# Last group's value product of a SwiGLU block as seven block products, in a planned single-core kernel

## The chip, the cores and the metric

The kernel runs on one core of a Trainium2 chip. The metric is the device time of one execution in microseconds (us); the time of a kernel is the median of several such executions.

## What is computed

Attention with two kinds of heads, and behind it a SwiGLU block on its output. The reference, cut to what matters:

```python
batch, n_heads, seq, head_dim = (4, 8, 768, 64)
n_sink, window = (4, 64)                     # heads 0, 2 and 6: causal
keep = causal & (is_sink | in_win)           # the other five heads
a = softmax(where(mask, q @ k.T / 8, -1e9))
attn_out = a @ v
x = attn_out.transpose(0, 2, 1, 3).reshape(3072, 512)
g = x @ w_gate                               # 512 x 1536
silu = g * (1.0 / (1.0 + np.exp(-g)))
val = x @ w_val                              # 512 x 1536
out = (silu * val) @ w_out                   # 1536 x 512
```

All inputs and the output are float32.

## The kernel before

The 3072 tokens are 24 tiles of 128, and four tiles make a group of 512 tokens: six groups, g = 0 to 5. Attention works on pairs of tiles: q and k are cast to float16 (`copy`, lines 206 on ACT and 208 on DVE and POOL, `recast`, line 212) and transposed by TensorE (line 473); then scores (line 567), exponentials on ACT (line 579), masks (line 587, DVE or POOL), values (line 597), the division by the row sums (lines 604 and 605, DVE), and a DMA that transposes the result into `xt`, the layout that the SwiGLU block takes.

For each group there are twelve blocks j of 128 of the 1536 columns. `gate` (line 759) makes four 512-wide matmuls into a PSUM bank, once with `wg_sb` (the gate) and once with `wv_sb` (the value, called vals). ACT takes the tanh of half the gate (line 765), and DVE makes two passes: `stt1` (line 769), sil = (tanh + 1) * gate, and `stt2` (line 775), h = 0.5 * sil * value, which goes as float16 into `h_sb`. `stt1` reads `sig` from SBUF and the gate from PSUM; `stt2` reads `sil` from SBUF and the value from PSUM.

The out projection h @ w_out is already done in 2x2 blocks with seven block products in all six groups (`seventh`, line 860: twelve 256-wide matmuls for each product). With A the blocks of h (token halves by column halves) and W those of w_out, it needs four sums of blocks of h (`hsum`, line 831, each in two parts, on DVE or POOL; named hs4.1.0 for group 4, sum 1, part 0) and four of w_out, made once (`wsum`, line 412). The products p1 to p7 of a group come together again in `gathered` (a copy at line 890, sums with a cell of `out_sb` at line 898); stores follow at lines 908, 911 and 919. The last group ends with its products in the order p1, p7, p6, first half of p2, p5, p4, second half of p2, the two halves of p3.

Nothing is scheduled at run time. The kernel's text adds tasks with their dependencies, and three tables, made beforehand by a planner, say what happens: `ORDER` (two base-62 digits for each task, in the order in which the tasks are issued; numbers of 3700 and above are matmuls that fill), `WAYS` (which of a task's engines takes it) and `SLOTS` (which buffer of a ring or which PSUM bank it uses). Each engine works through its own instructions in that order, and semaphores hold it until what it needs is there. The rings have 11 buffers `raw` (128x1024 float32, the landing place of the loads), 3 `sil`, 2 `sig`, 2 `xt`, and 8 PSUM banks that gates, values and products share.

The places that the change and the prediction touch:

Of the kernel before, what the change touches and what calls it, by code (L numbers as in the profile page):

```python
# [16 lines left out]
    "06000307090A0401081U0D1V1cy11W1X0C1d1f1e0B2021021g280g1i2229231h2B2A1j0m1r2C0h1Y1p1s2D1a0F1Z2N1q"  # L17
    "2X1b1k2E0G2O1l2W1t1m2F1u2L1x1v1w2f2M1n2g2c1y1oxk2h0n27242d25262e2l2i2m2G1z0E0y2H2I2P0z2Q2j8e2R2t"
    "8o0k8f112o2x8p8g302p108q2U312J0i132V8h2K8r2y050H8t8s8y8i8u2k983C8w8v8m323D8j2n2z3I0q8k9D8x991493"
    "3J8l9A3L8z8n94380l91903K96950o2Z9E929B3M979G2Y9F0I3N9C3U339H1C3R3V2a2q2r0j342b9h2s3S162u3O3W9c9i"  # L20
    "0r3T3X9j359d363b9I3P0J3E372v9J3Q3f3i1D2w9N9e0K1F3A9O9f3B3g2S3H9k0p179P3G0v9m9g393F9l9Q9n3h0s3Y3j"
    "9K3Z0u199r3u3a3c3n9R0x3l9s401G3k3m0w9L3o0L3d9M9S3v419o9u2T9t0M9T3p429U433w3q9v441A9p3r450R4C493e"
    "1B469q4A9X4H3y3s4B9Y9a479Z9V3t4D9b3x4Q4N4K9W4OAu9z480O4LAQ9y1H18AnA00tB2Av124RAz1EAw0P4EB0A1BE4Z"
    "B1Ap4V4Y4gB34FBH4GBF0NAxAq1Q1K4hBGAV5CArAkAWBIB41IAl0QAX1J15AY4eAy1S4IB7AZAm0SALAR3z4JAoB51MAs4d"
    "AS9wAt4f1RAM5DANB91TB69x5KBCB8BA4b5fBBAa0WBD5I4o4i4l4P4pA2A45l4m1LA34M5FAT0U1N5E4S5L1PAUAf4jA5A8"
    "1OAg4v5JAbAh4a4k4TAcAE5g4UA95n4y514q4c4zAAA60V4r0a6KACAB5o5GA7AF4WAdAD524n4sAGAiAeAK540TAj505T55"
    "4t5mAO4u5U5MAP565W4x5753AHBM4wBLBJBN5NAI5c5VAJ58595XBO4XBR5A5H5O5BBK5v5p5sBP5wBX5q5Y0YBQ600Z5r5Z"
    "5t5a0XBV5b6I5u6366BWCb6E6HBS645iCe5h6N67BY5PBTCC6O5QBbCD5R7O5d6PCM6wCc6v5xCd0cBZ68CECN71BcCF6JBa"
    "5SCP65BdCf5yCH72COCGBsBUCI73CJ69Bv6A5z5j0fBt6R616U74BuBi6V6e7RC7Bw0bBj6W5kBkCW6zCQ706B6CCX7SBlC8"
    "6D6SCAC96GBmC2CY7P6QCKC3CB6LCZ6T6x5e6yC4BnCLBhBqBoCa82626FBxBpBr7U6X7F6ZBy7GC0Bz0eCiCR6aC10d6Y7C"  # L30
    "7W6nCS75BeCT767XC5Bf776b6cBg6oDj6d7QDm7DC685DtDk7ED5DuDlCUD86gCVDvDUCk7VDeDnDVD6Cj78DwD7ClDXDWDf"
    "Dx79DA7LDY7HDPDgD9CgDQ7A80DR7B7b6kCmDBDh6lDCDSDi7c6MCh7Y6h817Z6p7jDyDT877a7I7J6q6mDK8883DzDD7K6f"
    "DoE07NDLCoDMDp6iCn86DEE16j89CsE2Cp6rCt7m7e7n6sDqDF7M7f7oCuDGDNCv7dDH7gCw6tCqDO6u7s7pCx7t7h7xDZ7i"
    "7q7T8D8ADa8G7rCyDb8H7k8E8NDI84Cz8B8F7uD07v8Y8I7wDc8C8J8ZDJ8T8W7y8Q8XEzDdCr8K8L8UEX8MDr8OEw7lD1Ex"
    "8P8REyF9D2D4F0F6D38SF1F7DsEh8VF88aE58bE6FJFAFB8cE7FE8dFCEiErEj7zE3FDF2E8FFFGFLFHFIEkFKEYEcF3EaEA"
    "EdElF4EZEBEbE4EmE9EEG9EnF5EeFOEoFMEfEDEsEuEtGMEvEFFNEgEpEGGJEHGKGLESEqEIGEG4GFGGGHG5FPEJGIG6G7EC"
    "GTG8GCGUGAEOGBEKETEVEUGiEWGWGjGVELFuENFTGNFxFvGXERGlFSGkFpEMFwFVGYFqGDFQEPFrGOFyFsGPFRGQGREQFUGZ"
    "GdGmFWFYGaFXFzFtFbGSGbG0GeG1G2FaFiG3FZFcGfGpGcGgFdFeGrGhFlGqFfFjFgFmGsFnGnFhFkGzGoGtFoGuGvGxH7Gy"
    "H3GwH8H9H0H1H4HAH6H2HDHBH5HCHGHEHFHHHI"
)  # L40
WAYS = (
    "000000000000000000000000000000000000000000000000000000000000222212202202222022110100101101110001"
    "212100001000000000000000210012022201011011000000000000001100222212001010000000000001000000000000"
    "001200002201000000000001000000001000000010000000000220120000000000010000002000000000000020000220"
    "000000100100000000200010000000000020000000000000000000000000210002120000000000100000210001001000"
    "002202020020000001001000000002000000000000000021002000000000000000010001000202220000000001000000"
    "000010010000010002212100000010010000000100000000000000000000000000000000000000000000000000000000"
    "000000000000000000000000000000000000000000001100001100000000000000000000000000000000000000000000"
    "000000000000000000000000000000000000000110000000000000000000000000000000000000000000000000000000"
    "000000000000000000010001100011000000000001000000000000000000000000000000000000000000000000000000"  # L50
    "000000001000000000000000000000110000000000000000000000000000000000000000000000000000000000000011"
    "010000110000000000010000000000000000000000000000000000000000000000000000000000000000101000000000"
    "00011001011000000"
)
# [1073 lines left out]
```

## Time and profile before

| what | value |
|---|---|
| median of 3 executions | 239.04 us (238.83 to 239.19) |
| profiled execution | 239.03 us |
| span in its profile | 237.2 us |
| PE (TensorE matmuls) busy | 230.5 us, 97% |
| DVE (VectorE) busy | 194.5 us, 82% |
| ACT (ScalarE) busy | 141.2 us, 59% |
| POOL (GpSimd) busy | 110.6 us, 47% |
| moved by DMA | 40.73 MB |

The profile is one execution seen by the hardware profiler. Its times are in us. PE is the sequence of matmuls and PEld that of weight loads, which overlap them; SP issues most of the DMAs. A row of the timeline gives the start, the duration, the engine, the line of the kernel, the operation with its output and inputs, and in brackets how long the engine had waited and for what. A row of a group of instructions gives their busy time, the mean duration in ns, and the idle time before them with what ended it. A row of stretches gives the busy time of PE, PEld, DVE, ACT and POOL, each with its instructions, then the granted clock of TensorE (1.00 is full speed), the busy share of the DMA engines and GB/s.

### The profile page before, as it was taken

How to read it: one execution, taken by the hardware profiler on the slowest of the kernel's cores; microseconds unless marked ns; L12 is line 12 of the kernel's file. 1: busy time of each engine (PE TensorE's matmuls, PEld its weight loads, DVE VectorE, ACT ScalarE, POOL GpSimd, SP SyncE). 2: the span in 40 equal slices, each digit the busy share in tenths (PEclk: the TensorE clock that was granted, in tenths of full speed). 3: DMA queues.
4: the chain of work that ended last, by engine and by line, in shares of the span. 5: the costliest groups of instructions: out<-in, count | busy, mean ns of one | idle time of the engine just before them, and what ended most of it. 6: DMA issues, size and time to landing. Idle time of an engine off the chain costs nothing.

```text
span 237.2 us, 5639 instructions
## 1 busy us (share of the span) xinstructions
PE 230.5 (97%) x2211; PEld 146.0 (62%) x2211; DVE 194.5 (82%) x362; ACT 141.2 (59%) x217; POOL 110.6 (47%) x132
## 2 busy tenths in 40 slices
PE   7899999999999999999999999999999999999994
PEld 2577865655457778655464557766555565557883
DVE  2689999998999699698968989786969867788873
ACT  3699999889599879839575485384242232231010
POOL 7386577937484940998600550884000000525500
PEclk9999999999999999999999999999999999999999
DMA  6999999999999999999798124011620000220044
GB/s 173 351 343 366 326 346 356 358 350 296 271 238 165 236 291 182 289 164 188 196 171 207 34 48 87 4 22 20 203 44 0 3 0 0 87 92 1 20 183 155
DMA packets 67194, 40.73 MB, mean 172 GB/s; under 512 B 25184, under 2 KB 61024, under 8 KB 67168
## 3 DMA queue, kind: packets, MB, share of 16 engines
q1 hardware_dynamic: 65248, 37.50, 63.4%
q10 hardware_dynamic: 1920, 2.88, 3.3%
q8 instruction: 17, 0.28, 0.5%
q14 instruction: 9, 0.07, 0.1%
HBM read 28.31 MB, written 6.29 MB: 146 GB/s over the span
## 4 chain that ended last, share of the span: by engine, by line
PE 92%; DVE 3%; DMA 2%; ACT 1%; issue 0%; DVEq 0%
PE banks L759 51%; PE banks L860 23%; PE banks L567 8%; PE banks L597 6%; PE banks L473 2%; DMA raw<-in_q_dram 2%; PE banks L621 1%; DVE wt_sb L412 1%; DVE sil L769 1%; ACT hq L206 0%; PE banks L321 0%; DVE kT L208 0%; DVE hq L212 0%; DVE qT L208 0%; DVE xb L605 0%; DVE h_sb L775 0%
## 5 line engine op out<-in xcount | busy, mean ns | idle before, releaser
L765 ACT ACTIVATE sig<-banks 128x512 f32<-128x512 f32 (+1 forms) x76 | 42.7, 574 | 54.6 <-PE banks L759 47.5
L759 PE MATMUL banks<-xt,wg_sb 128*128 128x512 f16 (+1 forms) x304 | 71.4, 368 | 0.5 <-DVE sil L769 0.5
L759 PE MATMUL banks<-xt,wv_sb 128*128 128x512 f16 (+1 forms) x304 | 70.9, 368 | 0.0
L579 ACT ACTIVATE e<-banks 128x1024 f16<-128x1024 f32 (+2 forms) x68 | 59.5, 910 | 15.0 <-PE banks L567 6.3
L769 DVE SCALAR_TENSOR_TENSOR sil<-sig,banks 128x512 f32<-128x512 f32 (+1 forms) x76 | 48.8, 655 | 14.3 <-ACT sig L765 13.6
L775 DVE SCALAR_TENSOR_TENSOR h_sb<-sil,banks 128x512 f16<-128x512 f32 (+1 forms) x76 | 48.9, 655 | 2.8 <-PE banks L759 1.8
L860 PEld LDWEIGHTS <-h_sb 128*128 128x128 f16 x420 | 40.4, 98 | 8.5
L759 PEld LDWEIGHTS <-wv_sb 128*128 128x128 f16 x304 | 28.6, 98 | 26.9
L759 PEld LDWEIGHTS <-wg_sb 128*128 128x128 f16 x304 | 28.1, 98 | 27.2 <-issue 0.8
L587 POOL TENSOR_TENSOR e<-e,m 128x640 f16<-128x640 f16 (+1 forms) x17 | 28.0, 1655 | 19.8 <-ACT e L579 19.4
L831 POOL TENSOR_TENSOR h_sb<-h_sb 128x768 f16<-128x768 f16 x13 | 21.2, 1640 | 22.5 <-DVE hs_sb L831 16.7
L898 DVE TENSOR_TENSOR out_sb<-banks,out_sb 128x512 f32<-128x512 f32 x37 | 25.1, 688 | 7.4 <-PE banks L860 7.0
L860 PE MATMUL banks<-wt_sb,h_sb 128*128 128x256 f16 x216 | 26.2, 273 | 0.0
L831 POOL TENSOR_TENSOR hs_sb<-h_sb 128x768 f16<-128x768 f16 x3 | 4.9, 1639 | 45.1 <-PE banks L860 41.2
L860 PE MATMUL banks<-wo_sb,h_sb 128*128 128x256 f16 x204 | 25.1, 273 | 0.0
L597 PEld LDWEIGHTS <-e 128*128 128x128 f16 x472 | 18.0, 97 | 5.8 <-DVE e L587 0.2
L567 PEld LDWEIGHTS <-kT 64*128 64x128 f16 x472 | 14.4, 94 | 9.3 <-issue 8.7
L567 PE MATMUL banks<-qT,kT 64*128 64x128 f16 x472 | 19.7, 218 | 0.2 <-ACT qT L206 0.2
L597 PE MATMUL banks<-vt,e 128*128 128x65 f16 x472 | 19.7, 193 | 0.1
L206 ACT CAST hq<-raw 128x1024 f16<-128x1024 f32 (+1 forms) x16 | 14.7, 936 | 5.2 <-DMA raw<-in_q_dram 3.2
L605 DVE TENSOR_TENSOR xb<-banks,rc 128x512 f16<-128x512 f32 x24 | 16.6, 692 | 0.8
L208 POOL CAST vt<-raw 64x512 f16<-64x512 f32 x23 | 14.0, 607 | 2.3 <-DMA raw<-in_v_dram 1.3
(64 smaller groups left out, 192.9 us busy)
## 6 DMA issues: line engine op xcount, KB each, us to landing
raw<-in_v_dram SPq DMA_DIRECT2D x12, 512.0 KB, 5.8
raw<-in_q_dram SPq DMA_DIRECT2D x8, 512.0 KB, 6.2
raw<-in_k_dram SPq DMA_DIRECT2D x8, 512.0 KB, 5.3
raw<-in_moe_w_gate_dram SPq DMA_DIRECT2D x6, 512.0 KB, 8.6
raw<-in_moe_w_val_dram SPq DMA_DIRECT2D x6, 512.0 KB, 8.2
raw<-in_moe_w_out_dram SPq DMA_DIRECT2D x6, 512.0 KB, 7.9
out_dram<-out_sb SPq DMA_DIRECT2D x6, 512.0 KB, 4.4
raw<-in_q_dram SPq DMA_DIRECT2D x8, 256.0 KB, 6.4
```

The source lines that it names most:

```text
L567: nc.tensor.matmul(sc[:, c:c + n, :], weights, moving, start=first, stop=last)
L579: nc.scalar.activation(out=to, in_=src, func=AF.Exp, scale=scale)
L587: ENG[task().way].tensor_tensor(out=ev, in0=ev, in1=mm, op=ALU.mult)
L597: nc.tensor.matmul(avs[t][:, odd, n * 66:n * 66 + 65], ee, vv, start=(m == 0), stop=(m == len(bl) - 1))
L605: nc.vector.tensor_tensor(out=xb.rearrange("p n o d -> p o n d"), in0=av[:, :, :, 0:64], in1=rc.to_broadcast([128, 2, 4, 64]), op=ALU.mult)
L759: nc.tensor.matmul(ps, wsb[:, kk, j * 128:(j + 1) * 128], xt[:, kk, c[0]:c[1]], start=(kk == 0), stop=(kk == 3))
L765: nc.scalar.activation(out=sg[g, j, c], in_=gs[g, j, c], func=AF.Tanh, scale=0.5)
L769: nc.vector.scalar_tensor_tensor(out=sl[g, j, c], in0=sg.pop((g, j, c)), scalar=1.0, op0=ALU.add, in1=gs.pop((g, j, c)), op1=ALU.mult)
L775: nc.vector.scalar_tensor_tensor(out=hs[g, j][:, c[0]:c[1]], in0=sl.pop((g, j, c)), scalar=0.5, op0=ALU.mult, in1=vs.pop((g, j, c)), op1=A ...
L831: ENG[T_hs[g, x][part].way].tensor_tensor(out=to, in0=a, in1=b, op=op)
L860: nc.tensor.matmul(rooms[g, p][:, x, lo:hi], left[:, j, 128 * x:128 * x + 128], right[:, j, lo:hi], start=(on is None and (j == 0 if apart ...
L898: nc.vector.tensor_tensor(out=cell(*to), in0=room, in1=plus, op=ALU.add)
```

## The change

In the last group the twelve value blocks, 48 matmuls of 512 columns, are replaced by seven block products. The value product is cut into 2x2 blocks: the 512 tokens in halves, the 512 inner features in halves, and the 1536 columns in a lower and an upper half, of which pair s (0 to 2) takes two blocks of 128 each. For the whole of w_val four sums of weight blocks are made once (`vsum`, tasks vw1 to vw4, two parts each of 128x768 float16), and for the group four sums of blocks of x (`xsum`, tasks xs5.1 to xs5.4, 128x512 float16). Both lie in buffers of the ring `raw`.

Each of the three pairs then has seven products of four 256-wide matmuls (`w_product`, tasks wp5.s.p). Products 1, 6, 7 and 4 add up in one PSUM bank (X), product 2 has a bank (Y), products 5 and 3 share a third (Z). Between them five copies per pair (`w_copy`, on ACT or DVE) take the partial sums r1, u2, u3, y2 and c21 out to float32 cells in buffers of `raw`, and three additions (`w_add`) complete c11 (both inputs in cells, on POOL or DVE), c22 and c12 (a cell and the bank Z, on DVE). The second SwiGLU pass of the group is the new `stt2_w` (line 1114 of the changed kernel): 0.5 * sil * value, where the value is now such a cell instead of a PSUM bank.

The three tables are made anew, so other things move too: eight block sums of h go from DVE to POOL, half of the first q is cast by POOL instead of ACT, five of the large masks go from DVE to POOL and three of the small ones the other way, and in the last group the copy of the first half of c11 goes from DVE to ACT and its store from ACT's queue to SP's. Lines up to about 1030 are one higher in the changed kernel.

The diff; of the tables it shows a line of one:

```diff
-    "06000307090A0401081U0D1V1cy11W1X0C1d1f1e0B2021021g280g1i2229231h2B2A1j0m1r2C0h1Y1p1s2D1a0F1Z2N1q"
...
+    "0602030700090A04081U1V0D011cxl1W1X0C1d1f1e0B20211g280g1h1i2229232B2A1j0m1r2C0h1Z1p1s2D1b0F1Y2N1q"
...
 WAYS = (
...
 SLOTS = (
...
+    WINO = (5,)
+    HJ = DFF // 2
+    v_sums, x_sums, w_rooms, low_cells, high_cells = {}, {}, {}, {}, {}
+    VB = {(y, c): wv_sb[:, 2 * y:2 * y + 2, HJ * c:HJ * c + HJ]
+          for y in range(2) for c in range(2)}
+
+    def vsum(i, kk):
+        if kk == 0:
+            v_sums[i] = buf("raw", [128, 1024], FP, "raw").bitcast(FH)[
+                :, 0:2 * HJ].rearrange("p (k n) -> p k n", k=2)
+        a, b = {1: (VB[0, 1], VB[0, 0]), 2: (VB[1, 1], v_sums.get(1)),
+                3: (VB[1, 1], VB[0, 1]), 4: (VB[1, 0], v_sums.get(2))}[i]
+        ENG[T_vw[i][kk].way].tensor_tensor(
+            out=v_sums[i][:, kk], in0=a[:, kk], in1=b[:, kk], op=ALU.subtract)
+
+    T_vw = {}
+    for i in range(1, 5) if WINO else []:
+        T_vw[i] = []
+        for kk in range(2):
+            before = {2: T_vw[1], 4: T_vw.get(2, [])}.get(i, [])[kk:kk + 1]
+            T_vw[i].append(P.add(
+                f"vw{i}.{kk}", ["DVE", "POOL"], (lambda i=i, kk=kk: vsum(i, kk)),
+                deps=[y for n in range(6) for y in T_w["v", n]] + before,
+                takes=[] if kk else ["raw"], after=T_vw[i][:1]))
+
+    def x_blocks(g):
+        return {(x, y): xts[g][:, 2 * y:2 * y + 2, 256 * x:256 * x + 256]
+                for x in range(2) for y in range(2)}
+
+    def xsum(g, i):
+        A = x_blocks(g)
+        if i == 1:
+            x_sums[g] = buf("raw", [128, 1024], FP, "raw").bitcast(FH).rearrange(
+                "p (i k n) -> p i k n", i=4, k=2)
+        Z = x_sums[g]
+        a, b, op = {1: (A[1, 0], A[1, 1], ALU.add), 2: (Z[:, 0], A[0, 0], ALU.subtract),
+                    3: (A[0, 0], A[1, 0], ALU.subtract),
+                    4: (A[0, 1], Z[:, 1], ALU.subtract)}[i]
+        ENG[T_xs[g, i].way].tensor_tensor(out=Z[:, i - 1], in0=a, in1=b, op=op)
+
+    W_ON = {1: "X", 6: "X", 7: "X", 4: "X", 2: "Y", 5: "Z", 3: "Z"}
+
+    def w_product(g, s, p):
+        A = x_blocks(g)
+        left = {1: A[0, 0], 2: A[0, 1], 4: A[1, 1], }.get(p)
+        if left is None:
+            left = x_sums[g][:, {5: 0, 6: 1, 7: 2, 3: 3}[p]]
+        right = {1: VB[0, 0], 2: VB[1, 0], 3: VB[1, 1], }.get(p)
+        if right is None:
+            right = v_sums[{4: 4, 5: 1, 6: 2, 7: 3}[p]]
+        on = g, s, W_ON[p]
+        begins = p in (1, 2, 5)
+        if begins:
+            w_rooms[on] = buf("gv", [128, 2, 256], FP, "gv")
+        for m in range(2):
+            at = 128 * (2 * s + m)
+            for kk in range(2):
+                nc.tensor.matmul(
+                    w_rooms[on][:, m], right[:, kk, at:at + 128], left[:, kk],
+                    start=(begins and m == 0 and kk == 0), stop=(kk == 1),
+                    skip_group_check=True)
+
+    def w_cell(g, s, name):
+        tile_, at = {"r1": (low_cells, 0), "c11": (low_cells, 0), "y2": (low_cells, 1),
+                     "c21": (low_cells, 1), "u2": (high_cells, 0), "c12": (high_cells, 0),
+                     "u3": (high_cells, 1), "c22": (high_cells, 1)}[name]
+        if name in ("r1", "u2"):
+            tile_[g, s] = buf("raw", [128, 1024], FP, "raw").rearrange(
+                "p (x m n) -> p x m n", x=2, m=2)
+        return tile_[g, s][:, at]
+
+    def w_copy(g, s, name):
+        to = w_cell(g, s, name)
+        copy(T_wc[g, s, name], to, w_rooms[g, s, "Y" if name == "y2" else "X"])
+
+    def w_add(g, s, name):
+        to = w_cell(g, s, name)
+        other = w_cell(g, s, "y2") if name == "c11" else w_rooms[g, s, "Z"]
+        ENG[T_wc[g, s, name].way].tensor_tensor(out=to, in0=other, in1=to, op=ALU.add)
+
+    def stt2_w(g, j):
+        hs[g, j] = h_sb[:, g % 2, j]
+        val = (low_cells if j < NK else high_cells)[g, j % NK // 2][:, :, j % 2]
+        nc.vector.scalar_tensor_tensor(
+            out=hs[g, j].rearrange("p (x n) -> p x n", x=2),
+            in0=sl.pop((g, j, (0, 512))).rearrange("p (x n) -> p x n", x=2),
+            scalar=0.5, op0=ALU.mult, in1=val, op1=ALU.mult)
+
+    T_xs, T_wp, T_wc = {}, {}, {}
+
+    def tasks_of_wino(g, xs):
+        first = T_first_x[g]
+        for i in range(1, 5):
+            T_xs[g, i] = P.add(
+                f"xs{g}.{i}", ["DVE", "POOL"], (lambda i=i: xsum(g, i)),
+                deps=xs + {2: [T_xs.get((g, 1))], 4: [T_xs.get((g, 2))]}.get(i, []),
+                takes=[] if i > 1 else ["raw"], after=[T_xs[g, 1]] if i > 1 else [])
+            P.uses(first, "xt", T_xs[g, i])
+        sum1 = T_xs[g, 1]
+        P.uses(sum1, "raw", T_xs[g, 2], T_xs[g, 4])
+        for s in range(NK // 2):
+            w_lo, w_hi = list(T_w["v", s]), list(T_w["v", s + 3])
+
+            def product(p, deps, s=s):
+                t = T_wp[g, s, p] = P.add(
+                    f"wp{g}.{s}.{p}", ["PE"], (lambda: w_product(g, s, p)),
+                    deps=deps, takes=["gv"] if p in (1, 2, 5) else [])
+                if p in (1, 2, 4):
+                    P.uses(first, "xt", t)
+                else:
+                    P.uses(sum1, "raw", t)
+                if p >= 4:
+                    P.uses(T_vw[{4: 4, 5: 1, 6: 2, 7: 3}[p]][0], "raw", t)
+                return t
+
+            def copied(name, deps, s=s):
+                T_wc[g, s, name] = P.add(
+                    f"wy{g}.{s}.{name}", ["ACT", "DVE"], (lambda: w_copy(g, s, name)),
+                    deps=deps, takes=["raw"] if name in ("r1", "u2") else [])
+                return T_wc[g, s, name]
+
+            def added(name, deps, s=s):
+                T_wc[g, s, name] = P.add(
+                    f"w{'a' if name == 'c11' else 'b'}{g}.{s}.{name}",
+                    ["POOL", "DVE"] if name == "c11" else ["DVE"],
+                    (lambda: w_add(g, s, name)), deps=deps)
+                return T_wc[g, s, name]
+
+            p1 = product(1, xs + w_lo)
+            r1 = copied("r1", [p1])
+            p6 = product(6, [r1, T_xs[g, 2]] + T_vw[2])
+            u2 = copied("u2", [p6])
+            p7 = product(7, [u2, T_xs[g, 3]] + T_vw[3])
+            u3 = copied("u3", [p7])
+            p4 = product(4, [u3] + T_vw[4])
+            p2 = product(2, xs + w_lo)
+            y2 = copied("y2", [p2, r1])
+            P.uses(p2, "gv", y2)
+            c11 = added("c11", [y2])
+            c21 = copied("c21", [p4, c11])
+            P.uses(p1, "gv", c21)
+            p5 = product(5, [T_xs[g, 1]] + T_vw[1])
+            c22 = added("c22", [p5, u3])
+            p3 = product(3, [c22, T_xs[g, 4]] + w_hi)
+            c12 = added("c12", [p3])
+            P.uses(p5, "gv", c12)
+
     for g in range(NG):
         w = SIZES[g] * 128
         xs = [T_xe[t] for t in range(FIRST[g], FIRST[g + 1])]
         T_h = {}
+        if g in WINO:
+            tasks_of_wino(g, xs)
         for j in range(NJ):
             parts = [(0, 256), (256, 512)] if g == 0 and j < HALVES else [(0, w)]
             for c in parts:
@@ -1042,18 +1192,28 @@
                            (lambda g=g, j=j, c=c: tanh(g, j, c)), deps=[a], takes=["sig"])
                 s1 = P.add(f"stt1 {g}.{j}.{c[0]}", ["DVE"],
                            (lambda g=g, j=j, c=c: stt1(g, j, c)), deps=[th], takes=["sil"])
+                was = [T_p[g - 2, p] for p in ((6, 7) if j < NK else (3, 4))] if g > 1 else []
+                was += T_hs[g - 2, 4] if g > 1 and j < NK else []
+                P.uses(a, "gv", s1)
+                P.uses(th, "sig", s1)
+                if g in WINO:
+                    cells = [T_wc[g, j % NK // 2, y]
+                             for y in (("c11", "c21") if j < NK else ("c12", "c22"))]
+                    s2 = P.add(f"stt2 {g}.{j}.{c[0]}", ["DVE"],
+                               (lambda g=g, j=j: stt2_w(g, j)), deps=[s1] + cells + was)
+                    T_h.setdefault(j, []).append(s2)
+                    P.uses(s1, "sil", s2)
+                    P.uses(T_wc[g, j % NK // 2, "r1" if j < NK else "u2"], "raw", s2)
+                    P.uses(T_first_x[g], "xt", a)
+                    continue
                 v_ = P.add(f"vals{g}.{j}.{c[0]}", ["PE"],
                            (lambda g=g, j=j, c=c: gate(g, j, c, wv_sb, vs)),
                            deps=xs[c[0] // 128:c[1] // 128] + [T_w["v", j // 2][j % 2]],
                            takes=["gv"])
-                was = [T_p[g - 2, p] for p in ((6, 7) if j < NK else (3, 4))] if g > 1 else []
-                was += T_hs[g - 2, 4] if g > 1 and j < NK else []
                 s2 = P.add(f"stt2 {g}.{j}.{c[0]}", ["DVE"],
                            (lambda g=g, j=j, c=c: stt2(g, j, c)), deps=[s1, v_] + was)
                 T_h.setdefault(j, []).append(s2)
-                P.uses(a, "gv", s1)
                 P.uses(v_, "gv", s2)
-                P.uses(th, "sig", s1)
                 P.uses(s1, "sil", s2)
                 P.uses(T_first_x[g], "xt", a, v_)
         if g < SEVENS:
```

Where it stands in the order. On DVE, around group 5's product 5 of the stretch before the end, before: `h_sb` is written by `stt2` (line 775) from `sil` and a PSUM bank.

```order
L775 SCALAR_TENSOR_TENSOR h_sb_92<-sil_3274,banks_87 128x512
L769 SCALAR_TENSOR_TENSOR sil_3320<-sig_3316,banks_87 128x512
L775 SCALAR_TENSOR_TENSOR h_sb_92<-sil_3320,banks_87 128x512
L898 TENSOR_TENSOR out_sb_94<-banks_87,out_sb_94 128x2x256
L769 SCALAR_TENSOR_TENSOR sil_3353<-sig_3318,banks_87 128x512
L831 TENSOR_TENSOR hs_sb_93<-h_sb_92 128x768
L775 SCALAR_TENSOR_TENSOR h_sb_92<-sil_3302,banks_87 128x512
```

On DVE in the changed kernel, the gates of group 5 towards the end: `raw_...` are the cells.

```order
L1114 SCALAR_TENSOR_TENSOR h_sb_92<-sil_3331,raw_2997 128x512
L1109 TENSOR_TENSOR raw_3090<-banks_87,raw_3090 128x512
L770 SCALAR_TENSOR_TENSOR sil_3363<-sig_3345,banks_87 128x512
L770 SCALAR_TENSOR_TENSOR sil_3377<-sig_3360,banks_87 128x512
L1114 SCALAR_TENSOR_TENSOR h_sb_92<-sil_3363,raw_3050 128x512
L1114 SCALAR_TENSOR_TENSOR h_sb_92<-sil_3377,raw_2997 128x512
L770 SCALAR_TENSOR_TENSOR sil_3390<-sig_3380,banks_87 128x512
L1114 SCALAR_TENSOR_TENSOR h_sb_92<-sil_3325,raw_3044 128x512
L1114 SCALAR_TENSOR_TENSOR h_sb_92<-sil_3390,raw_3042 128x512
```

The second pass reads a cell in SBUF where it read a bank; all twelve of line 1114 stand behind the last line 776 of group 4.

On POOL, sums of h blocks of groups 4 and 5 before, with the semaphores that each waits on:

```order
L831 TENSOR_TENSOR hs_sb_93<-h_sb_92 128x768 [waits DVE_49,PE_49]
L831 TENSOR_TENSOR hs_sb_93<-h_sb_92 128x768 [waits DVE_49]
L831 TENSOR_TENSOR h_sb_92<-h_sb_92 128x3x256 [waits Pool_49]
L831 TENSOR_TENSOR h_sb_92<-h_sb_92 128x3x256 [waits DVE_49,PE_49]
L831 TENSOR_TENSOR h_sb_92<-h_sb_92 128x3x256
```

And in the changed kernel, from its addition c11 of pair 2 on:

```order
L1109 TENSOR_TENSOR raw_3050<-raw_3050 128x512 [waits Activation_49]
L832 TENSOR_TENSOR h_sb_92<-h_sb_92 128x3x256 [waits Pool_49]
L832 TENSOR_TENSOR h_sb_92<-hs_sb_93,h_sb_92 128x3x256 [waits PE_49,Pool_49]
L832 TENSOR_TENSOR h_sb_92<-hs_sb_93,h_sb_92 128x3x256 [waits PE_49]
L832 TENSOR_TENSOR h_sb_92<-h_sb_92 128x3x256 [waits PE_49,Pool_49]
L832 TENSOR_TENSOR hs_sb_93<-h_sb_92 128x768 [waits DVE_49,PE_49]
L832 TENSOR_TENSOR h_sb_92<-h_sb_92 128x3x256 [waits Pool_49] x2
```

Of the sums of h of groups 4 and 5 POOL makes seven before; in the changed kernel it makes eleven between the last `stt2` of group 4 and product 5 of group 5, and the addition c11 of pair 2 among them. In that stretch PE's order is, from group 3's product 5 on: that product, the gate of block 7 of group 5, products 4 and 3 of group 3, gates 6 and 2, product 3 of pair 2, gates 9, 4 and 3, products 1 and 2 of group 4, gates 11 and 10, products 5 and 6, gate 5, products 7, 4 and 3, and product 1 of group 5.

More of the change, by code (lines that the diff above doesn't have):

```diff
@@ L22 @@
[L22 to L26, printed above, removed]
@@ new lines @@
+    "903J9B9I3L97959C380l99983M9D9E0o2Z9A9M9J3N9F9O2Y9N0j3K9K3U3R9P331C3V2a2q2r0r342b9p2u3S169k2s0I9q"
+    "3T359l9r3O3W3P369m9V0J1D379Q9W3b3Q3X9s399X0K1F2v9t3f3i3g3E2w3A9n3F0p179R9z3j9S3h0s3Y9o3Z199Y3aA0"
+    "0t3n3G1G3l0L3o9u3cA13d9v9a3u0u3H3m9T3e3k9b9Z3v400x9c3p0MA22T9U413q429w0v3B43A31A9f443r0S3x45494C"
+    "3w469g9x4H4D9h479i159y4A3s9j9d0O3t4B4Q4K4Y9e4N48Ax4OA7B0A64L4VBMAy4M4E4RAzB70w0P4FB8BCBNA9B918Ad"
+    "BOB1BP124e1BBABQBD1K0Q1H4ZB21IB5Ae4g4G5CAvBB1EAgAf0RB35gAY4hAhBEAsA8B44JATAtAZAu1SBF5D0NAwBH5I3z"
@@ L63 @@
+    "242432902733610247485231201140241160251061061041230270061204823644"
 )
```

72 lines of the change are left out of this document (36 added, 36 removed).

## The prediction

> **What bounds the kernel now.** I read the busy shares first, then what TensorE (PE) waited for, then the chain of work that ended last. The page:
>
> ```profile
> span 237.2 us, 5639 instructions
> ...
> PE 230.5 (97%) x2211; PEld 146.0 (62%) x2211; DVE 194.5 (82%) x362; ACT 141.2 (59%) x217; POOL 110.6 (47%) x132
> ...
> PE 92%; DVE 3%; DMA 2%; ACT 1%; issue 0%; DVEq 0%
> ```
>
> All waits of PE's matmuls (engine and line that waited, who ended it, us in total, times, longest):
>
> ```profile
> PE banks L321 <- POOL ident L234: 1.4, 1, 1.4
> PE banks L473 <- DVE hq L212: 0.8, 1, 0.8
> PE banks L759 <- DVE sil L769: 0.5, 1, 0.5
> PE banks L567 <- ACT qT L206: 0.2, 1, 0.2
> ```
>
> PE is the bound, and after the first 20 us it waits once, for 0.5 us. So work taken from PE is worth its whole time, as long as no other engine becomes late. The same profile by stretches (busy us of PE, PEld, DVE, ACT, POOL, with instructions) shows who is next:
>
> ```profile
> 180.00:190.00 10.00, 10.00 (x60) 5.72 (x59) 8.62 (x15) 1.79 (x3) 0.00 (x0) 1.00 0.01 2
> ...
> 200.00:210.00 10.00, 10.00 (x61) 5.76 (x59) 8.39 (x14) 2.34 (x4) 4.84 (x3) 1.00 0.15 54
> 210.00:220.00 10.00, 10.00 (x65) 6.24 (x64) 8.26 (x15) 2.76 (x5) 3.23 (x2) 1.00 0.14 53
> ```
>
> DVE is second, ACT and POOL are mostly idle there. DVE's true pace is better than its busy time says. Its operations on 128x512 start 0.60 us apart when they follow each other: six rows of the timeline, of which the first and the last are
>
> ```profile
> 206.59 0.69 DVE L898 TENSOR_TENSOR out_sb<-banks,out_sb 128x512 f32<-128x512 f32 x1
> ...
> 209.58 0.68 DVE L775 SCALAR_TENSOR_TENSOR h_sb<-sil,banks 128x512 f16<-128x512 f32 x1
> ```
>
> (209.58 - 206.59) / 5 = 0.598 us. So 15 operations in 10 us are 9.0 us of work.
>
> The one late wait of PE tells most for this change. The timeline around it:
>
> ```profile
> 59.43 1.04 POOL L208 CAST hq<-raw 128x1024 f16<-128x1024 f32 x1 [1.46 <-DMA raw<-in_q_dram]
> 59.53 1.54 DVE L412 TENSOR_TENSOR wt_sb<-wo_sb 128x512 f16<-128x512 f16 x2
> ...
> 61.00 1.27 DVE L769 SCALAR_TENSOR_TENSOR sil<-sig,banks 128x512 f32<-128x512 f32 x2
> 61.73 0.38 PE L759 MATMUL banks<-xt,wg_sb 128*128 128x512 f16 x1 [0.50 <-DVE sil L769]
> ```
>
> and the durations of line 412 (min/median/max in ns):
>
> ```profile
> L412 DVE TENSOR_TENSOR wt_sb<-wo_sb x3: 411/414/1212, 59.5 to 62.8; 128x512 f16<-128x512 f16 x3
> ```
>
> The DVE sum that began 0.1 us behind a POOL cast took 1212 ns instead of 411: it ended at 60.75, 0.28 us after the cast's end at 60.47. Its two inputs both lie in SBUF. A DVE operation of that kind does not run beside a POOL operation; the later one is held until the other is done. DVE came 0.8 us late, and that became PE's 0.5 us. The reverse order costs POOL:
>
> ```profile
> 39.34 0.69 DVE L587 TENSOR_TENSOR e<-e,m 128x1024 f16<-128x1024 f16 x1
> ...
> 39.76 1.16 POOL L208 CAST wg_sb<-raw 128x1024 f16<-128x1024 f32 x1 [1.18 <-DMA raw<-in_moe_w_gate_dram]
> ```
>
> The cast takes 1.16 us instead of 1.04 us. The overlap was 40.03 - 39.76 = 0.27 us, so 0.12 us of it was lost and 0.15 us of the hand-over was hidden.
>
> **The products (PE).** The chain that ended last prices matmuls by contiguous pieces:
>
> ```profile
> 175.57 5.18 PE banks L759 x24
> ...
> 220.62 13.11 PE banks L860 x120
> ```
>
> A 512-wide matmul is 5.18/24 = 0.2158 us, a 256-wide one 13.11/120 = 0.1093 us. Removed are 12 x 4 = 48 of the first, 10.36 us; added are 3 x 7 products of 4 of the second, 84 x 0.1093 = 9.18 us. Difference -1.18 us, all on the path. The shorter matmuls pay no extra for their weight loads, since line 860's run at half the time of the long ones.
>
> **The extra evictions.** 15 copies and 9 additions; ACT takes 8 of the copies, DVE 7 copies and 7 additions, POOL 2 additions.
>
> ```profile
> L206 ACT COPY raw<-banks 128x512 f32<-128x512 f32 x1 | 0.6, 585 | 9.4 <-PE banks L860 9.4
> L208 DVE COPY out_sb<-banks 128x512 f32<-128x512 f32 x2 | 1.4, 684 | 0.0
> ```
>
> ACT: 8 x 0.585 = 4.7 us in some 30 us where it is busy a quarter: hidden. DVE: 14 x 0.60 = 8.4 us, against which eight of its block sums of h go to POOL. Products that add into one bank wait for the copy between them. In the new order other matmuls stand in between; the least is 0.86 + 0.44 = 1.3 us between the third pair's products 1 and 6, against a copy of 0.6, so they cost nothing; without that cover each copy costs PE its 0.6 us.
>
> **The sums of weights and x.** Seven of the eight weight sums are POOL's, one DVE's; of the x sums three are POOL's. At the 1.62 us of POOL's sums of that size (row below) the seven are 11.3 us, five of them done before group 5 begins, on an engine that is busy 47% of the span: nothing. Their buffers are taken from the ring of the loads, two of eleven while the last loads are still to come; I give that nothing, since those loads are for tiles much later. The x sums need the last transpose of x, behind the normalization of its tile:
>
> ```profile
> L604 DVE RECIPROCAL rc<-banks 128x8 f32<-128x8 f32 x24 | 4.9, 206 | 4.2 <-PE banks L597 3.8
> ```
>
> ```profile
> L605 DVE TENSOR_TENSOR xb<-banks,rc 128x512 f16<-128x512 f32 x24 | 16.6, 692 | 0.8
> ```
>
> ```profile
> xt<-xb SPq DMA_TRANSPOSE x16, 2.9
> ```
>
> 0.21 + 0.69 + 2.9 = 3.8 us after PE's last attention product it has landed, and eight 512-wide groups of group 4 (8 x 0.863 = 6.9 us) stand before the first block product: 3.1 us to spare for what DVE has queued ahead.
>
> **The start.** POOL casts half of the first q instead of ACT. The two casts were
>
> ```profile
> 5.19 1.15 ACT hq L206 x2
> ...
> 8.37 0.70 DVE hq L212
> ```
>
> in the chain, but the chain goes on to the second pair's cast at 8.37, which the change does not move. Nothing, +-0.3 us, other small shifts in the order of the first 60 us included. At the very end one half store moves from ACT's queue to SP's, ahead of the last two:
>
> ```profile
> 233.55 1.00 SPq L908 DMA_DIRECT2D out_dram<-out_sb  x2
> ```
>
> Its issue takes 0.5 us, and half of product 3 (6 x 0.1093 = 0.66 us) lies between it and the next: nothing, 0.5 us at most.
>
> **The second SwiGLU step.** This is the large term. For the last group stt2 multiplied sil (SBUF) by a PSUM bank; now it multiplies sil by a cell in SBUF (new stt2_w, line 1114 of the changed kernel). All twelve thereby become operations with two inputs in SBUF. In the new order all twelve stand behind group 4's last stt2, and in the same stretch POOL has eleven block sums of h (lines 832) and one addition. The stretch is bounded on both sides: the first of these POOL sums needs that last stt2 and group 3's product 5, and the last one, with the last stt2_w before it, feeds group 5's product 5. POOL's prices:
>
> ```profile
> 204.24 3.24 POOL L831 TENSOR_TENSOR hs_sb<-h_sb 128x768 f16<-128x768 f16 x2 [41.25 <-PE banks L860]
> ...
> L412 POOL TENSOR_TENSOR wt_sb<-wo_sb 128x512 f16<-128x512 f16 x3 | 3.5, 1159 | 0.1
> ```
>
> PE's work in it, counted from the order: 9 gates x 0.863 + 10 products x 1.31 + one block product 0.44 = 21.3 us. POOL: 11 x 1.62 + 1.16 = 19.0 us, which fits beside PE. DVE: 32 operations x 0.60 = 19.2 us, which fits too. But if the twelve stt2_w exclude POOL, their 12 x 0.60 = 7.2 us and POOL's 19.0 us lie one behind the other: 26.2 us, **4.9 us** more than PE has.
>
> Bounds: with 0.15 us of each hand-over hidden as at 39.76, and 12 to 21 hand-overs, 1.8 to 3.1 us come off, so 1.8 us is the low end. High end: every stt2_w waits half a POOL sum, 12 x 0.81 = 9.7 us, less DVE's slack of 21.3 - 19.2 = 2.1: 7.6 us. I take 4.9, the plain count. Queued behind a held stt2_w are the stt1 and the evictions on DVE that free PSUM banks, so PE's gates and products wait for them at once, and product 5 for POOL's last sum.
>
> The Trainium skill, page "SBUF — State Buffer", section "Who interferes with whom", says that a VectorE instruction with two SBUF inputs contends with a GpSimd instruction that reads SBUF, and that the one that starts second is blocked for the whole of the other. By that rule nothing of a hand-over is hidden, and the time would be 242.8 us or more; the trace's held DVE operation agrees (1212 ns against 411), its held cast was delayed by less than the rule has it (0.12 us of 0.27).
>
> **Sum.** The profiled execution took 239.03 us, 237.2 of span and 1.8 around it; the median is 239.04, so nothing is to be corrected. 239.03 - 1.18 + 4.9 = **242.8 us**; the forecast's own range is 237.85 + 1.8 = 239.7 to 237.85 + 7.6 = 245.4.
>
> **Rivals.**
> 1. *The exclusion does not hold for these operations (faster).* The held one was a float16 sum against a cast; stt2_w reads two float32 operands against float16 sums. Then stt2_w runs at 0.60 us beside POOL, and only PE's saving is left: 237.9 us; 237.4 if the 0.5 us of 61.73 goes too, 238.4 if the dense stretch (DVE 19.2 of 21.3 us) costs PE some 0.5 us. For it: no such pair is in this trace. Against: the three sums of line 412 differ in nothing but the POOL cast beside one of them. Its point of decision is whether line 1114 shows durations near 0.68 us while POOL works. Chance 0.24.
> 2. *The exclusion holds but mostly hides.* If DVE always gets its turn between two POOL sums and hand-overs hide, some 1.2 us is left, and the saving is eaten: 237.85 + 1.2 = 239.05 us, the same. Chance 0.06.
> 3. *The chains of copies stall PE (slower).* Products 1, 6, 7, 4 of one pair add into one PSUM bank, with a copy after each. If DVE or ACT is behind by more than the 1.3 us at the tightest place, each of the 15 copies and 9 additions costs PE up to its 0.6 us. With a quarter of them late, 6 x 0.6 = 3.6 us: 237.85 + 3.6 = 241.4. Against: ACT is idle three quarters of the time there. Chance 0.06.
>
> **How the numbers follow.** The forecast gets 0.64. About 0.2% (0.48 us) is what a measurement of this kernel can tell from no change: below 238.56 is faster, above 239.52 slower. Slower: 0.64 + 0.06 = 0.70, faster 0.24, same 0.06. The range must reach into the first rival, since that holds more than 2 in 10, and takes most of the forecast's own: 237.5 to 244.6.
>
> **What would show it.** Line 1114: some of twelve durations well over 0.7 us, each ending shortly after a POOL sum's end; POOL's block sums over 1.65 us; PE waits of several us in total in the last 40 us, ended by DVE's stt1 or evictions and by POOL's sums before group 5's product 5. PE's busy time for the last group's value product should be 9.2 us. The forecast is wrong if line 1114 stays at 0.68 us while POOL is working, or if PE's new waits come before the first stt2_w.

## The result, and the profile after

The changed kernel takes 247.28 us (247.25 to 247.46, four executions) against 239.0 us before: 1.0348 times as long, 95% interval 1.033 to 1.0366. It is slower by 8.3 us, by more than the forecast's 3.8 us, and above its range of 237.5 to 244.6 us.

The page of the changed kernel:

```profile
span 245.5 us, 5760 instructions
PE 231.6 (94%) x2247; PEld 150.2 (61%) x2247; DVE 207.3 (84%) x366; ACT 147.8 (60%) x230; POOL 150.3 (61%) x151
PE 73%; DVE 16%; issue 4%; ACT 3%; DMA 2%; SPq 1%; DVEq 0%
```

The last line is the chain that ended last, by engine: PE's part fell from 92% to 73%, and DVE's rose from 3% to 16%. PE now waits in places where it never did. Its waits (engine and line that waited, who ended it, us in total, times, longest), without those of the start and two of 0.2 us:

```profile
PE banks L861 <- DVE out_sb L899: 2.4, 3, 1.2
PE banks L861 <- DVE sil L770: 1.7, 1, 1.7
PE banks L760 <- DVE xb L606: 1.6, 1, 1.6
PE banks L760 <- DVE sil L770: 1.4, 1, 1.4
...
PE banks L598 <- DVE e L588: 0.6, 1, 0.6
```

DVE ends all of them, and two places are behind them. The waits for `out_sb` and for `sil` lie between 210 and 232 us, where the prediction had looked; those for `xb` and for a masked e lie between 165 and 172 us, where it had not.

**The late place.** The new second pass, with the minimum, median and maximum of its twelve durations, and then as a group (busy us, mean ns):

```profile
L1114 DVE SCALAR_TENSOR_TENSOR h_sb<-sil,raw x12: 674/1369/2119, 204.6 to 231.3; 128x512 f16<-128x512 f32 x12
```

```profile
L1114 DVE SCALAR_TENSOR_TENSOR h_sb<-sil,raw 128x512 f16<-128x512 f32 x12 | 15.1, 1280 | 0.0
```

The shortest takes the 0.68 us of any operation of this size, the median is twice that; eight of the twelve are longer than 0.7 us. The timeline of DVE and POOL shows why:

```profile
206.32 3.23 POOL L832 TENSOR_TENSOR hs_sb<-h_sb 128x768 f16<-128x768 f16 x2 [12.61 <-PE banks L861]
...
208.32 1.78 DVE L1114 SCALAR_TENSOR_TENSOR h_sb<-sil,raw 128x512 f16<-128x512 f32 x1
209.51 2.09 POOL L832 TENSOR_TENSOR h_sb<-h_sb 128x768 f16<-128x768 f16 x1
210.03 1.41 DVE L899 TENSOR_TENSOR out_sb<-banks,out_sb 128x512 f32<-128x512 f32 x2
```

The second pass begins at 208.32, while POOL's sum runs until 209.55 (206.32 + 3.23), and ends 0.55 us after that, at 210.10. POOL's next sum begins at 209.51 and is held in its turn: 2.09 us instead of 1.64. The eviction at 210.03, which reads PSUM, runs beside POOL at 0.7 us for each of its two. So one engine waits for the other alternately, and DVE's row counts the hold as busy time. That is the trap in the table of stretches (PE, PEld, DVE, ACT, POOL):

```profile
220.00:230.00 10.00, 7.15 (x56) 5.29 (x55) 10.00 (x10) 1.75 (x3) 8.90 (x5) 1.00 0.01 2
```

DVE is "busy" for all of 10 us, with ten instructions where it can do sixteen.

What it cost PE is read from its own timeline. The stretch of the prediction runs from the gate behind group 3's product 5 to group 5's product 5:

```profile
206.02 1.03 PE L760 MATMUL banks<-xt,wg_sb 128*128 128x512 f16 x4
...
214.48 1.89 PE L760 MATMUL banks<-xt,wg_sb 128*128 128x512 f16 x8 [1.40 <-DVE sil L770]
...
234.00 1.47 PE L861 MATMUL banks<-wt_sb,hs_sb 128*128 128x256 f16 x12
```

234.00 - 206.02 = 28.0 us for the 21.3 us of matmuls that the prediction had counted there: 6.7 us lost, where it had put 4.9. The six waits of PE in this stretch sum to 5.6 us. The rest is at their ends: groups of matmuls that follow each other without a wait overlap by 0.17 us in the timeline (the gate at 206.02 lasts 1.03 us, and the next product begins 0.86 us after it), and with each wait this overlap is lost too, 1.0 us in all.

**The early place.** Between 163 and 172 us both engines work on operands in SBUF at the same time, too:

```profile
163.10 1.83 POOL L832 TENSOR_TENSOR h_sb<-h_sb 128x768 f16<-128x768 f16 x1
163.77 1.70 DVE L588 TENSOR_TENSOR e<-e,m 128x1024 f16<-128x1024 f16 x1 [0.34 <-ACT e L580]
164.89 2.08 POOL L832 TENSOR_TENSOR hs_sb<-h_sb 128x768 f16<-128x768 f16 x1
...
165.53 0.41 PE L598 MATMUL banks<-vt,e 128*128 128x65 f16 x8 [0.64 <-DVE e L588]
165.99 1.32 DVE L588 TENSOR_TENSOR e<-e,m 128x640 f16<-128x640 f16 x1
...
168.77 1.95 POOL L1043 TENSOR_TENSOR raw<-wv_sb,raw 128x768 f16<-128x768 f16 x1
169.27 1.87 DVE L832 TENSOR_TENSOR h_sb<-h_sb 128x768 f16<-128x768 f16 x1
...
172.03 1.02 PE L760 MATMUL banks<-xt,wg_sb 128*128 128x512 f16 x4 [1.59 <-DVE xb L606]
```

Masks of 0.68 and 0.48 us take 1.70 and 1.32, sums of h of 0.55 take up to 1.87. POOL has three sums of h there, two of which were DVE's before, and a half of a weight sum. The division by the row sums comes late behind them, and PE waits 0.6 and 1.6 us. No second pass of the last group is involved.

### The profile page after: what moved, and what is told of

The parts are those of the page before. It is cut to its first block, busy times and chain, and to the rows that moved or that the text cites. A ratio compares the mean times of both kernels' runs of the same rounds, so it can differ in the third digit from the quotient of the medians.

```text
span 245.5 us, 5760 instructions
## 1 busy us (share of the span) xinstructions
PE 231.6 (94%) x2247; PEld 150.2 (61%) x2247; DVE 207.3 (84%) x366; ACT 147.8 (60%) x230; POOL 150.3 (61%) x151
## 4 chain that ended last, share of the span: by engine, by line
PE 73%; DVE 16%; issue 4%; ACT 3%; DMA 2%; SPq 1%; DVEq 0%
PE banks L760 39%; PE banks L861 18%; PE banks L568 6%; PE banks L598 5%; DVE h_sb L1114 4%; PE banks L1088 3%; DVE sil L770 3%; DMA raw<-in_q_dram 2%; DVE h_sb L776 2%; DVE out_sb L899 2%; ACT e L580 2%; DVE xb L606 1%; PE banks L474 1%; DVE e L588 1%; DVE raw L1109 1%
## 5 line engine op out<-in xcount | busy, mean ns | idle before, releaser
L760 PE MATMUL banks<-xt,wv_sb 128*128 128x512 f16 (+1 forms) x256 | 59.6, 366 | 0.2 <-DVE h_sb L776 0.2
L776 DVE SCALAR_TENSOR_TENSOR h_sb<-sil,banks 128x512 f16<-128x512 f32 (+1 forms) x64 | 40.9, 650 | 7.4 <-PE banks L760 6.7
L588 POOL TENSOR_TENSOR e<-e,m 128x1024 f16<-128x1024 f16 (+1 forms) x19 | 34.6, 1820 | 14.8 <-ACT e L580 14.4
L760 PEld LDWEIGHTS <-wv_sb 128*128 128x128 f16 x256 | 23.7, 98 | 22.5 <-issue 0.5
L832 POOL TENSOR_TENSOR h_sb<-h_sb 128x768 f16<-128x768 f16 x14 | 25.0, 1791 | 0.2
L832 POOL TENSOR_TENSOR hs_sb<-h_sb 128x768 f16<-128x768 f16 x6 | 10.6, 1766 | 15.8 <-PE banks L861 13.3
L598 PE MATMUL banks<-vt,e 128*128 128x65 f16 x472 | 19.2, 193 | 0.8 <-DVE e L588 0.6
L207 ACT CAST hq<-raw 128x1024 f16<-128x1024 f32 (+1 forms) x16 | 15.5, 968 | 4.9 <-DMA raw<-in_q_dram 2.9
L209 POOL COPY vt<-vt 2x330 f16<-2x330 f16 x16 | 7.4, 462 | 15.0 <-issue 14.5
```

The lines of the kernel that those rows point to most:

```text
L588: ENG[task().way].tensor_tensor(out=ev, in0=ev, in1=mm, op=ALU.mult)
L598: nc.tensor.matmul(avs[t][:, odd, n * 66:n * 66 + 65], ee, vv, start=(m == 0), stop=(m == len(bl) - 1))
L760: nc.tensor.matmul(ps, wsb[:, kk, j * 128:(j + 1) * 128], xt[:, kk, c[0]:c[1]], start=(kk == 0), stop=(kk == 3))
L776: nc.vector.scalar_tensor_tensor(out=hs[g, j][:, c[0]:c[1]], in0=sl.pop((g, j, c)), scalar=0.5, op0=ALU.mult, in1=vs.pop((g, j, c)), op1=A ...
L832: ENG[T_hs[g, x][part].way].tensor_tensor(out=to, in0=a, in1=b, op=op)
```

## The experiments

Two theories were set against each other. By the exclusion theory, DVE operations that read two operands in SBUF are held while POOL works, and all of the loss is such holds, in two places. By the load theory, DVE simply has too much to do: the change gives it seven copies and seven additions more. Beside them stands the prediction's third rival, the copy chains, by which PE waits for the copies between block products.

**Sums taken from POOL and given to DVE.** These moves pull the theories apart, since they add load and take away overlap. First the early place, then the late one, then both; the edits are in the table of engines, here written out by task:

```diff
-hs2.4.1 hs3.1.1 hs3.3.1 vw2.0: POOL
+hs2.4.1 hs3.1.1 hs3.3.1 vw2.0: DVE
```

> The changed kernel with four block sums that POOL makes between 163 and 171 us (sums 1 and 3 of group 3, one half each, sum 4 of group 2, one half, one half of weight sum 2) given to DVE, where they stand in the same place of the order. Exclusion theory: DVE has four more operations of 0.55 us, but its masks and sums there (822, 1704, 1322, 1286 and 1873 ns) go back to their own 0.5 to 0.7 us, some 4 us of DVE time; PE's waits between 164 and 173 us, 2.9 us, go: 244.4 us (243.8 to 245.2). Load theory (DVE simply has too much to do): four operations more make it later: 248 to 249.5 us.

245.76 us, 1.5 us less than the changed kernel; the operations of DVE are back at 0.5 to 0.8 us. It is about half of what was expected. The four sums now stand ahead of the mask that PE waits for:

```profile
PE banks L598 <- DVE e L588: 1.2, 1, 1.2
```

The wait of 1.6 us is gone and the one of 0.6 us has grown to 1.2. DVE got more work and the kernel became faster, which the load theory excludes; the size was left to a better order (below).

```diff
-hs4.1.1 hs4.1.0 hs4.3.1 hs4.3.0 hs4.2.0 hs4.2.1 hs4.4.0 hs5.1.0 hs4.4.1 hs5.3.0 hs5.1.1 wa5.2.c11: POOL
+hs4.1.1 hs4.1.0 hs4.3.1 hs4.3.0 hs4.2.0 hs4.2.1 hs4.4.0 hs5.1.0 hs4.4.1 hs5.3.0 hs5.1.1 wa5.2.c11: DVE
```

> The changed kernel with the eleven block sums of groups 4 and 5 and the addition that POOL makes between 206 and 230 us given to DVE. Exclusion theory: all twelve of line 1114 show 0.68 us; DVE wins back 7.2 us of holds and pays 11 x 0.47 + 0.6 = 5.8 us for the sums, so PE's late waits of 6.6 us shrink to 2 to 4 us, ended by a DVE that is now merely full: 244.0 us (242.5 to 245). Load theory: DVE only gets 5.8 us more to do in a stretch where it is late already: 252 us or more.

244.60 us, 2.7 us less, with twelve operations more on DVE in the tightest stretch. The twelve second passes:

```profile
L1114 DVE SCALAR_TENSOR_TENSOR h_sb<-sil,raw x12: 679/683/686, 204.6 to 228.8; 128x512 f16<-128x512 f32 x12
```

No POOL operation, no hold. PE's late waits that remain are those of a DVE that is now full: it has no gap longer than 0.1 us between 208 and 233 us.

> Both moves of the two kernels before in one. Exclusion theory: the two gains add, 247.3 - 2.9 - 3.3 = 241.1 us (239.5 to 242.5). Load theory: 253 us or more.

243.52 us. The two gains add up to 4.2 us, and 3.8 us come off; the 241.1 us of the expectation had taken the early gain as 2.9, which the first of these runs had not given.

**One SBUF operand less.** The second pass leaves out the value:

```diff
-        nc.vector.scalar_tensor_tensor(
...
-            scalar=0.5, op0=ALU.mult, in1=val, op1=ALU.mult)
+        nc.vector.tensor_scalar(
+            out=hs[g, j], in0=sl.pop((g, j, (0, 512))),
+            scalar1=0.5, scalar2=None, op0=ALU.mult)
```

> The changed kernel with the second pass of the last group reading sil alone (0.5 * sil as a tensor_scalar; the product with the value is left out, though the value is still computed). Nothing else moves: the same POOL sums, the same copies and additions. Exclusion theory: an operation with one SBUF input isn't held, line 1114's place shows 0.7 us or less twelve times, the late waits of 6.6 us go and the early ones of 2.9 us stay: 240.7 us (240.2 to 241.5). Theory of the copy chains, and load theory: only what the twelve operations get shorter by comes off, below 4 us of DVE and less of PE: 244.5 to 247.3 us.

244.92 us, far from the 240.7 of the exclusion theory as it was put there, and inside the other theories' band. The row says what happened:

```profile
L1113 DVE TENSOR_SCALAR h_sb<-sil x12: 409/1236/1853, 204.6 to 228.9; 128x512 f16<-128x512 f32 x12
```

The form takes 0.41 us where it runs free, quicker than the 0.68 us of the second pass, and it is held as well. So "two inputs in SBUF" was too narrow. Either a quicker form like this one (the next expectation calls it a form at double pace) is excluded too, or every operation between SBUF and SBUF is. The next run decides it, with a slow form on one SBUF input in the place of the second pass:

```diff
+        nc.vector.tensor_reduce(
+            out=hs[g, j], in_=sl.pop((g, j, (0, 512))).unsqueeze(2),
+            axis=mybir.AxisListType.X, op=ALU.max)
```

> As the run with sil alone, but in another form of instruction: the second pass is a tensor_reduce over a last axis of one element (the factor and the product with the value are left out). One SBUF input, as there, but a form that isn't run at double pace. If what excludes POOL is two SBUF inputs or a double-pace form, these twelve are not held, last 0.7 us each, and the time is 240.7 us (240.2 to 241.8). If every operation between SBUF and SBUF is excluded, they are held for as long as the twelve of the run with sil alone were, and the time is 245 us or more.

240.77 us, 6.5 us less than the changed kernel with the same copies, additions and POOL sums:

```profile
L1113 DVE TENSOR_REDUCE h_sb<-sil x12: 674/680/687, 204.7 to 224.4; 128x512 f16<-128x512 f32 x12
```

Twelve operations as long as the unheld second pass, and not one held. So a quick form on one SBUF input is excluded as well as an operation on two, and a slow form on one is not. The load theory and the copy chains are out for the late place: both would have kept the 247 us. The Trainium skill has the rule in this wider form on the page "SBUF — State Buffer", section "Who interferes with whom": copies, casts and tensor_scalar can enter a mode that takes the ports shared with GpSimd, tensor_reduce cannot on this chip. Both runs agree with it (median 1236 ns against 680); the prediction had used only the clause on two inputs. The two runs compare one instruction of each kind, so they do not separate whether its pace or the instruction itself decides.

**The operand alone, in the kernel before.** Only the second pass of the last group is changed there:

```diff
+        if g == NG - 1:
+            vs.pop((g, j, c))
+            sil = sl.pop((g, j, c))
+            nc.vector.scalar_tensor_tensor(
+                out=hs[g, j][:, c[0]:c[1]], in0=sil, scalar=0.5, op0=ALU.mult,
+                in1=sil, op1=ALU.mult)
+            return
```

> The kernel before with one thing of the change alone: the second pass of the last group reads two SBUF operands (0.5 * sil * sil; the product with the value is left out, though its 48 matmuls still run into their banks). No block products, no copies, the old order. POOL makes seven block sums of groups 4 and 5 there. Exclusion theory: some of the twelve last 1 to 2 us, POOL's sums beside them up to 2.1 us, and PE waits that the kernel before doesn't have: 239.6 to 242 us. Load theory: DVE has as much to do as before and PE's banks come free earlier, so 239.0 us, or less.

242.67 us, 1.0165 times the time of before (1.013 to 1.0201), more than expected:

```profile
L778 DVE SCALAR_TENSOR_TENSOR h_sb<-sil x12: 680/684/2130, 195.3 to 224.9; 128x512 f16<-128x512 f32 x12
```

```profile
PE banks L759 <- DVE out_sb L905: 2.1, 1, 2.1
...
PE banks L867 <- DVE sil L769: 1.0, 1, 1.0
```

Only four of the twelve are held (1.22 to 2.13 us), since POOL does less there. Two of them, at 204.88 and 206.42 us, stand ahead of PE's wait of 2.1 us at 209.80, and a third, at 217.47, ahead of that of 1.0 us at 220.45. No block product, copy or new order is needed for 3.5 us.

**The operand back in PSUM.** Here the change keeps all its work and loses only the second SBUF operand: sil goes back into the gate's bank, which is kept until the second pass; the banks from there on are dealt out anew.

```diff
-        sl[g, j, c] = buf("sil", [128, 512], FP, "sil")[:, 0:c[1] - c[0]]
+        sl[g, j, c] = gs[g, j, c] if g in WINO else buf(
+            "sil", [128, 512], FP, "sil")[:, 0:c[1] - c[0]]
...
-                P.uses(a, "gv", s1)
+                if g not in WINO:
+                    P.uses(a, "gv", s1)
...
-                    P.uses(s1, "sil", s2)
+                    P.uses(a, "gv", s2)
```

> The changed kernel with sil of the last group written back into the gate's PSUM bank instead of an SBUF buffer, so that the second pass reads one operand in PSUM (sil) and one in SBUF (the cell). The bank is kept until then, so the banks are dealt out anew from there on; order and engines are as in the changed kernel, with all eleven late POOL sums and the addition. Exclusion theory: line 1114's place shows 0.7 us twelve times, POOL's sums 1.62 us, the late waits of 6.6 us go, the early 2.9 stay: 240.7 us (240.2 to 242, the upper end if banks become short). Load theory and the theory of the copy chains: unchanged, 247 us or more, since DVE does the same work in the same order.

240.59 us, 6.7 us less, as expected. The second pass, and PE's stretch from the gate behind group 3's product 5 to group 5's product 5:

```profile
L1115 DVE SCALAR_TENSOR_TENSOR h_sb<-banks,raw x12: 680/684/692, 204.6 to 224.2; 128x512 f16<-128x512 f32 x12
```

```profile
206.05 1.03 PE L760 MATMUL banks<-xt,wg_sb 128*128 128x512 f16 x4
...
227.36 1.47 PE L862 MATMUL banks<-wt_sb,hs_sb 128*128 128x256 f16 x12
```

227.36 - 206.05 = 21.3 us, PE's own work to a tenth. What is left above 238 us is the early place.

**The early place dealt out better.** A first try put three sums of h and both halves of a weight sum on DVE, one sum (hs2.4.1) in its old place and the other four halves behind the masks and the last tile's normalization:

> The kernel before this one with the early place mended too: the four sums between 163 and 171 us on DVE, and three of them and the DVE half of weight sum 2 behind the masks and the normalization of the last tile instead of ahead of them. Exclusion theory: both losses go, and what is left is the PE time that the block products save: 239.0 - 1.2 = 237.9 us (237.5 to 238.8), faster than the kernel before. Load theory: slower than the kernel before this one.

239.62 us, 1.0012 times the time of before (1.0000 to 1.0023): no faster. One wait is left:

```profile
172.30 1.02 PE L760 MATMUL banks<-xt,wv_sb 128*128 128x512 f16 x4 [1.62 <-DVE h_sb L777]
```

The four moved halves stood ahead of the second pass that frees PE's next bank. So they were moved behind it, and three of them (hs3.3.1 and both halves of weight sum 2, one of which DVE makes in the changed kernel) went to POOL, behind a sum on DVE that holds them until DVE has nothing between SBUF and SBUF to do. The edit against the changed kernel, written out by task:

```diff
-hs2.4.1: POOL; hs3.1.1 hs3.3.1 vw2.0: POOL, vw2.1: DVE, all ahead of mask23.0
+hs2.4.1: DVE; hs3.1.1: DVE, hs3.3.1 vw2.0 vw2.1: POOL, all behind stt2 4.6
```

> The run with sil in PSUM and the early place mended, with that place dealt out better: one half of sum 4 of group 2 and one half of sum 1 of group 3 on DVE, and behind that one POOL makes the half of sum 3 and both halves of weight sum 2, in a stretch in which DVE has no operation between SBUF and SBUF. PE's wait of 1.6 us at 172 us, for an operation of DVE that stood behind the four moved sums, should go. Exclusion theory: only the saving of the block products is left, 239.0 - 1.2 = 237.8 us (237.4 to 238.5), faster than the kernel before by 0.3 to 0.6%. If the block products do not save PE time: 239.0 us.

237.82 us, 0.9946 times the time of before on the same chip (0.9933 to 0.9958): faster than both kernels. Its span, the POOL sum that now begins behind DVE's, and all of PE's waits:

```profile
span 236.0 us, 5753 instructions
```

```profile
170.82 1.64 POOL L833 TENSOR_TENSOR h_sb<-h_sb 128x768 f16<-128x768 f16 x1 [7.68 <-DVE hs_sb L833]
```

```profile
PE banks L322 <- POOL ident L235: 1.4, 1, 1.4
PE banks L474 <- DVE hq L213: 0.9, 2, 0.7
```

Both waits belong to the first 10 us. The same order of the early place without sil in PSUM separates the two losses:

> The changed kernel with the early place alone dealt out in that way (order and engines of five sums), and the twelve operations of the last group with both operands in SBUF as the change has them. Exclusion theory: the early 2.9 us go and the late 6.6 us stay: 244.4 us (244.0 to 244.9). If the late waits followed from the early ones: 241 us or less.

244.42 us. So the early place is worth 247.28 - 244.42 = 2.9 us, the late one 247.28 - 240.59 = 6.7 us, and both together 247.28 - 237.82 = 9.5 us: they add up. (Beside these runs the kernel before took 239.1 to 239.2 us, against 239.0 beside the changed kernel, so such a difference is good to some 0.2 us.)

## Why the prediction was right or wrong

**The direction and the mechanism** were right: the second pass with both operands in SBUF is held by POOL's sums, in the stretch that the prediction named, and PE waits there for DVE's evictions and for sil. The prediction also named what would show it wrong, and one of these signs came: PE's waits at 165 and 172 us lie before the first second pass, at 204.6. The first rival (no exclusion, 237.9 us) fell with the median of 1369 ns. The second (it mostly hides) fell with the 6.7 us. The third (copy chains) fell with the runs that keep all copies and take 240.6 to 240.8 us.

**PE's saving of 1.18 us** was right as far as it can be seen. The block products run at the pace that was put for them; in the changed kernel

```profile
203.41 0.60 PE L1088 MATMUL banks<-xt,raw 128*128 128x256 f16 x4
203.85 1.03 PE L760 MATMUL banks<-xt,wg_sb 128*128 128x512 f16 x4
```

the gate begins 0.44 us after the product, and 21 x 0.44 = 9.2 us. The run without either loss, 237.82 us, is 1.0 to 1.6 us below the kernel before (the ends of its interval). Against that stand 1.18 us and the wait of 0.5 us at 61.73, which the first rival had as its better end and which that run no longer shows: 1.7 us in all. No run has the saving alone, without the new tables.

**The term of the second pass was mis-sized**: 4.9 us put, 6.7 measured, inside its bounds of 1.8 to 7.6. The count had DVE and POOL lie one behind the other, with POOL's end as the limit. In the trace PE waits not for POOL's sums but for what is queued on DVE behind a held pass. That is the picture of the upper bound, holds of 9.7 us less the 2.1 us that DVE had to spare, and both of its sizes were off. The run with the slow form on one input has the same order and banks and no hold. The pass that is the first held one in the changed kernel, and the last of the twelve, without holds and with them:

```profile
208.51 0.68 DVE L1113 TENSOR_REDUCE h_sb<-sil 128x512 f16<-128x512 f32 x1
...
224.40 0.68 DVE L1113 TENSOR_REDUCE h_sb<-sil 128x512 f16<-128x512 f32 x1
```

```profile
208.32 1.78 DVE L1114 SCALAR_TENSOR_TENSOR h_sb<-sil,raw 128x512 f16<-128x512 f32 x1
...
231.26 0.68 DVE L1114 SCALAR_TENSOR_TENSOR h_sb<-sil,raw 128x512 f16<-128x512 f32 x1
```

From the one to the other are 15.9 us without holds, with 0.16 us of gaps on DVE, and 22.9 us with them: 7.0 us more. The held passes are 12 x 1.280 - 12 x 0.68 = 7.2 us too long in all. So of the 2.1 us to spare only 0.5 us came off, since next to nothing of them lies between the held passes.

**The step that failed is the one on the sums of weights and the moved work.** The prediction gave the seven weight sums to "an engine that is busy 47% of the span: nothing", and counted the eight sums of h that go to POOL only as relief for DVE. It had just shown that POOL's work is not free where DVE has operands in SBUF, and then applied that to the second pass alone. (The eight are what is left of eleven that go to POOL and three that come back; by the two tables, some hundred tasks change their engine, more than the list under the change tells.) Masks and sums of h on DVE are of the same kind (the held operation in the trace of before was a float16 sum). The replanned order put POOL's sums of h and a weight sum beside two masks and two sums of h on DVE at 163 to 171 us. That was 2.9 us, and without it the time was 244.4 us, just inside the range. The range missed because it held the bounds of one unknown and no term for a second place.

In sum: 239.03 - 1.18 - 0.5 + 6.7 + 2.9 = 246.95 us, against 247.28 measured; 0.3 us stay unexplained.

## What to carry to other kernels

When work is moved to POOL, or a DVE operand from PSUM to SBUF, go through every stretch in which both engines work, and list DVE's operations there that read two SBUF operands, or are of a quick form between SBUF and SBUF like the tensor_scalar here: each such meeting costs the engine that begins second the rest of the other's operation. A share of busy time does not show it, since holds are counted as busy; compare the number of instructions and the longest of a group with its shortest. The remedies that worked here are an intermediate result left in PSUM and a POOL sum that starts behind a DVE sum; moving POOL's sums to DVE gave back 1.5 and 2.7 of 9.5 us.

## What the runs showed of the hardware beyond that

The exclusion is almost a full one, in both directions. The held second pass at 208.32 ended 0.55 us after POOL did, of the 0.68 us that it takes alone, so 0.13 us lay beside POOL's work; POOL's sum at 209.51 overlapped the pass by 0.59 us and became 0.45 us longer. That fits the 0.15 us that the kernel before had shown at 39.76. Part of it is only how the profile draws the ends: on one engine, too, DVE operations of 0.68 us start 0.60 us apart and POOL's sums of 1.64 us start 1.60 us apart, so that neighbours overlap by 0.08 and 0.04 us. And a quicker form is no help: the tensor_scalar at 0.41 us was held up to 1.85 us, while the tensor_reduce at 0.68 us ran free, and the kernel with the slower form was 4.2 us faster.
